# Local attention and two expert layers: pooled products ahead of the local maximum, more places for loads

## Chip, core and metric

One core of a Trainium2 chip runs the whole program. The metric is the device time of one execution in microseconds (us). The engines are TensorE (PE, with its weight loads as PEld), VectorE (DVE), ScalarE (ACT), GpSimd (POOL) and SyncE (SP), which only issues loads and stores.

## What is computed

Attention over 2 batches of 8 heads, 576 positions of 64 values, in two branches that are added: one over queries, keys and values averaged in fours (144 positions), one over the full sequence with a mask that leaves each query the keys less than 4 positions away. Then a dense two-layer block with a squared ReLU, then a mixture of 4 experts weighted by normalised probabilities.

```python
q_d = q.reshape(B, H, Sd, factor, D).mean(axis=3)      # k_d, v_d alike
out_up = np.repeat(sm_attn(q_d, k_d, v_d), factor, axis=2)
mask = np.abs(pos[:, None] - pos[None, :]) < factor
scores = np.where(mask, scale * np.matmul(q, k.transpose(0, 1, 3, 2)), -1e9)
attn = softmax(scores)
x = out_up + np.matmul(attn, v)                        # then (B*S, H*D)
x = (s * np.maximum(x @ w_in, 0) ** 2 + b) @ w_out
out = sum(p[:, e:e+1] * (np.maximum(x @ w1[e], 0) @ w2[e]) for e in range(4))
```

## The kernel before

The attention is cut into 16 units: a unit `u` is one pair of heads (64 + 64 partitions) in one half of the queries of one batch. The first half has 4 tiles of 64 queries, the second 5. Units 0 to 3 and 8 to 11 are first halves: they also load and transpose the keys of their pair and pool its keys and values, which the second-half units 4 to 7 and 12 to 15 use again. Each tile of queries sees a window of 72 keys.

A unit passes through steps, one loop turn apart. `a_step` transposes keys (line 494) and queries (line 512) on TensorE, copies them out of PSUM on ScalarE (kT, line 500; qz, line 519) and sums the queries in fours on VectorE (qd, line 526). `k_step` pools the keys on GpSimd (tk and kd, lines 539 and 541); `v_step` pools the values there (lines 474 and 475). `b_step` opens a PSUM bank with the mask (line 576), adds the local products (line 591), takes the negative local maximum on VectorE (ml, line 599), makes the pooled products (line 605 in first halves, line 615 in second halves) and their maximum (md, line 617), and has ScalarE compute all exponentials (`exps`, line 571). In first halves the pooled products lie in the same bank as the local ones, from column 360 on; in second halves one of two does, the other has a bank of its own. `norm_step` normalises on VectorE (lines 630 to 635), `c_step` transposes the probabilities (line 657, copied out at line 660), `d_step` multiplies them with the values (lines 678 and 685) and joins both branches (lines 694 and 701), and `x_step` splits the sum into two parts for the next layer (lines 713 and 715). There are five PSUM banks for all of these steps.

One loop turn `i` takes its steps in the order b(i-1), a(i), k(i), d(i-3), c(i-2), x(i-3), norm(i-1), v(i-1). Between them stand steps of weight conversion (`prep`: ScalarE at lines 157 and 196, VectorE at lines 161, 167, 175, 186, 199) and, once four units are done, products of the first dense layer (line 316). `keep_warm` adds products on zeros (line 361) whose result nobody reads; their number is fixed by `fill`. The order on each engine is then made by a planner from these priorities and a cost model, except on GpSimd, where it is the order as written. The planner also sets the waits: any two accesses to one PSUM bank by different engines are put in order, whatever columns they touch.

Loads are issued by SyncE in one queue. Turn `i` ends with the keys and queries of unit i+2 (kn, three places; qn, line 443, two places), the values to be pooled of unit i (v4, line 420, one place; in the trace this tile is called v), and the values in windows (vn, lines 458 and 465, three places). Weights are loaded by `load_next` (line 122) into two places.

After the attention the two layers run with TensorE as their pace: dense blocks to about 300 us, experts to the end.

Of the kernel before, what the change touches and what calls it, by code (L numbers as in the profile page):

```python
# [8 lines left out]
F32 = mybir.dt.float32  # L9
# [4 lines left out]
ALU = mybir.AluOpType  # L14
AX = mybir.AxisListType
# [7 lines left out]
def attn_moe_moe_kernel(  # L23
# [14 lines left out]
    nc = tc.nc  # L38
    B, H, S, D = q.shape
# [4 lines left out]
    TQ = 64  # L44
    NTQ = S // TQ
    HALVES = 2
    MX = (NTQ + 1) // 2
# [3 lines left out]
    FAC = 4  # L51
    SD = S // FAC
    ND = SD // 2
# [21 lines left out]
    def window(n):  # L75

        return min(max(n * TQ - FAC, 0), S - W)
# [307 lines left out]
    ap2 = actx.enter_context(tc.tile_pool(name="att2", bufs=2))  # L385
    rctx = ExitStack()
    ap4 = rctx.enter_context(tc.tile_pool(name="att4", bufs=1, side="right"))
# [10 lines left out]
    def unit(u):  # L398
        g, j = divmod(u, NP)
        b, hf = divmod(g, HALVES)  # L400
        return g, j, b, hf

    def tiles(hf):

        return (0, CUT) if hf == 0 else (CUT, NTQ - CUT)
# [6 lines left out]
    def bank():  # L412
        return psa.tile([P, 512], F32, tag="a", name="psa")


    def load_v4(u):
        if u < NU and unit(u)[3] == 0:
            g, j, b, hf = unit(u)
            v4 = ap4.tile([ND, 2, 2, FAC * D], F32, tag="v4", name="v4")
            nc.sync.dma_start(  # L420
                out=v4.rearrange("n a c f -> n (a c) f"),
                in_=v[b, 2 * j : 2 * j + 2].rearrange(
                    "a (c n r) d -> n (a c) (r d)", c=2, r=FAC
                ),
            )
            loaded["v4", u] = v4
# [10 lines left out]
    def load_q(u):  # L437
        if u < NU:
            g, j, b, hf = unit(u)
            n0, m = tiles(hf)  # L440
            gd = m * TQ // FAC
            qn = ap2.tile([MX * TQ // FAC, FAC, 2, D], F32, tag="qn", name="qn")
            nc.sync.dma_start(
                out=qn[:gd],
                in_=q[b, 2 * j : 2 * j + 2, n0 * TQ : (n0 + m) * TQ, :].rearrange(
                    "a (n r) d -> n r a d", r=FAC
                ),
            )
            loaded["q", u] = qn
# [101 lines left out]
    def b_step(u):  # L551

        g, j, b, hf = unit(u)
        n0, m = tiles(hf)
        gd = m * TQ // FAC
        qz, qd = st.pop(("q", u))
        kT = st["kT", j]
        kd = st["kd", j]
        pl = ap2.tile([P, MX, W], F32, tag="pl", name="pl")[:, :m]
        ml = ap2.tile([P, MX, 1], F32, tag="ml", name="ml")[:, :m]  # L560
        both = gd == GB
        pd = ap2.tile([P, 2, SD], F32, tag="pd", name="pd")
        md = ap2.tile([P, 2, 1], F32, tag="md", name="md")
        if both:
            pd, md = pd[:, :1], md[:, :1]
        else:
            pd, md = pd[:gd], md[:gd]
        sm = sums[u % 2]

        def exps(out, ps, m, total):  # L570
            nc.scalar.activation(
                out=out, in_=ps, func=ACTF.Exp, bias=m, scale=1.0, accum_out=total
            )

        ps = [bank()] + ([] if both else [bank()])
        last_pe["att"] = nc.tensor.matmul(
            ps[0][:, : m * W],
            identb.rearrange("p a q -> p (a q)"),
            mask[:, hf * 2 : hf * 2 + m].rearrange("p t w -> p (t w)"),
            start=True,  # L580
            stop=False,
        )
        for _ in range(fill[u] // 448):
            nc.tensor.matmul(
                ps[0][:, : m * W], idle[:, :P], idle[:, : m * W], start=False, stop=False
            )
        for t in range(m):
            k0 = window(n0 + t)
            for a in range(2):
                o = slice(a * D, a * D + D)  # L590
                last_pe["att"] = nc.tensor.matmul(  # L591
                    ps[0][a * TQ : a * TQ + TQ, t * W : t * W + W],
                    qz[o, t * TQ : t * TQ + TQ],
                    kT[o, k0 : k0 + W],
                    start=False,
                    stop=t == m - 1,
                )
        local = ps[0][:, : m * W].rearrange("p (t w) -> p t w", w=W)
        nc.vector.tensor_reduce(out=ml, in_=local, axis=AX.X, op=ALU.max, negate=True)
        pooled = [] if both else [ps[0][:gd, MX * W : MX * W + SD], ps[1][:gd, :SD]]  # L600
        if both:
            pooled = [ps[0][: 2 * gd, MX * W : MX * W + SD]]
            for a in range(2):
                o = slice(a * D, a * D + D)
                last_pe["att"] = nc.tensor.matmul(  # L605
                    ps[0][a * gd : a * gd + gd, MX * W : MX * W + SD],
                    qd[o, :],
                    kd[o, :],
                    start=True,
                    stop=True,  # L610
                )
        else:
            for a in range(2):
                o = slice(a * D, a * D + D)
                last_pe["att"] = nc.tensor.matmul(pooled[a], qd[o, :], kd[o, :], start=True, stop=True)  # L615
        for a in range(len(pooled)):
            nc.vector.tensor_reduce(
                out=md[:, a], in_=pooled[a], axis=AX.X, op=ALU.max, negate=True
            )
        for t in range(m):  # L620
            exps(pl[:, t], local[:, t], ml[:, t], sm[:, t])
        for a in range(len(pooled)):
            exps(pd[:, a], pooled[a], md[:, a], sm[: pd.shape[0], MX + a])
        st["p", u] = pl, pd
# [337 lines left out]
    def side_step():  # L962
# [5 lines left out]

    load_k(0)
    load_q(0)  # L970
    make_mask(0, 1)
    make_mask(1, CUT - 1)
    load_k(1)
    load_q(1)
    keep_warm(bank(), 0, 4096)
    pool_order = ExitStack()
    pool_order.enter_context(tc.manual_schedule(engines={mybir.EngineType.Pool}))
    steps = [
        (b_step, 1),
        (a_step, 0),  # L980
        (k_step, 0),
# [9 lines left out]
    for i in range(last + 1):  # L991
# [13 lines left out]
        for f, lag in steps:  # L1005
            u = i - lag
            if 0 <= u < NU:

                with tc.high_priority(ahead.get(f, 0)) if f in ahead and u < NP else nullcontext():
                    f(u)  # L1010
            if f is x_step and u >= 0 and u % NP == NP - 1:
                slots += l1_steps(0, u // NP) + l2_steps(0, u // NP)
                firsts.append(slots[-FC - KD])
                if u < NP:

                    for _ in range(3):
                        take_slot()
            if f in (k_step, c_step) and slots and i < last:
                take_slot()
            if f in (b_step, k_step, c_step, v_step):  # L1020
                side_step()
        load_k(i + 2)
        load_q(i + 2)
        load_v4(i)
        load_v(i)
        if i == 4:
# [105 lines left out]
```

## Time and profile before

| | |
|---|---|
| median of 3 runs | 696.87 us (695.46 to 697.39) |
| the profiled execution | 696.83 us |
| its span, first to last instruction | 695.0 us |
| TensorE busy | 683.0 us, 98% |
| VectorE busy | 404.8 us, 58% |
| ScalarE busy | 346.3 us, 50% |
| GpSimd busy | 101.2 us, 15% |
| mean granted TensorE clock | 0.993 |

The attention with what is woven into it ends at about 142 us. The share of TensorE's idle time is small, so it has to be looked for in places: the timeline gives each gap with what ended it, and the granted clock tells where TensorE ran at the lower of its two levels. A wait is put down to what came last.

### The profile page before, as it was taken

What the parts mean: (1) busy time and instruction counts of PE and PEld (TensorE: products, weight loads), DVE (VectorE), ACT (ScalarE), POOL (GpSimd) and SP (SyncE); (2) the same over time, 40 slices, a digit from 0 to 9 for tenths busy, and PEclk for the clock granted to TensorE, in tenths of its full rate; (3) what the DMA queues carried; (4) which work ended last, traced back from release to release, by engine and by line L of the source; (5) the groups of instructions that cost most, each with busy time, mean ns of one, the idle gap of its engine ahead of it and who ended that gap; (6) DMA issues with size and microseconds to landing.
All of it is one profiled execution on the core that took longest, in us unless ns stands there. A gap on an engine that the chain in (4) does not pass through costs nothing.

```text
span 695.0 us, 11964 instructions
## 1 busy us (share of the span) xinstructions
PE 683.0 (98%) x4788; PEld 620.2 (89%) x4788; DVE 404.8 (58%) x720; ACT 346.3 (50%) x846; POOL 101.2 (15%) x123
## 2 busy tenths in 40 slices
PE   9989999999999999999999999999999999999997
PEld 5768778899999999999899899999898988998996
DVE  1898847778862434496535636645546456455442
ACT  3768757777965666665534423433334233243220
POOL 4431332100000200103011201201211012010000
PEclk9999989999999999999999999999999999999999
DMA  8784635405410011010210201201101103011012
GB/s 179 200 206 102 110 83 159 141 6 192 166 64 1 0 32 46 16 32 1 62 31 31 70 21 56 67 32 38 54 31 62 30 32 91 3 60 31 1 61 75
DMA packets 54167, 46.43 MB, mean 67 GB/s; under 512 B 32224, under 2 KB 42720, under 8 KB 54112
## 3 DMA queue, kind: packets, MB, share of 16 engines
q1 hardware_dynamic: 54112, 45.67, 23.9%
q8 instruction: 37, 0.61, 0.4%
q14 instruction: 18, 0.15, 0.1%
HBM read 43.31 MB, written 2.36 MB: 66 GB/s over the span
## 4 chain that ended last, share of the span: by engine, by line
PE 92%; DVE 6%; ACT 2%; issue 1%; DVEq 0%; ACTq 0%
PE psm L316 43%; PE psx L863 25%; PE psx L316 13%; PE psa L361 3%; PE psa L657 1%; PE psa L685 1%; PE psa L591 1%; PE psa L678 1%; PE psa L512 1%; PE psa L615 1%; PE psa L494 1%; DVE cv L175 0%; DVE cv L186 0%; PE psa L605 0%; DVE cv L161 0%
## 5 line engine op out<-in xcount | busy, mean ns | idle before, releaser
L316 PE MATMUL psm<-w,h 128*128 128x512 f32 x864 | 208.7, 391 | 0.0
L316 PEld LDWEIGHTS psm<-w,h 128*128 128x128 f32 x864 | 158.5, 188 | 30.0
L863 PE MATMUL psx<-x,w 128*128 128x320 f32 (+1 forms) x768 | 117.8, 296 | 0.0
L863 PEld LDWEIGHTS psx<-x,w 128*128 128x128 f32 x768 | 109.3, 190 | 1.7
L259 POOL TENSOR_TENSOR sw<-raw 128x256 f32<-128x256 f32 x32 | 31.3, 1000 | 411.5 <-DMA raw<-in_moe_w_dram 245.4
L878 ACT COPY r<-psx 128x320 f32<-128x320 f32 (+1 forms) x96 | 38.0, 396 | 92.6 <-PE psx L863 92.2
L881 ACT ACTIVATE h<-r 128x320 fp32r<-128x320 f32 (+1 forms) x96 | 42.0, 444 | 83.6 <-DVE r L892 83.6
L934 DVE SCALAR_TENSOR_TENSOR acc<-psm,pr,acc 128x512 f32<-128x512 f32 x63 | 47.2, 749 | 58.0 <-PE psm L316 58.0
L863 PE MATMUL psx<-t,w 128*128 128x320 f32 (+1 forms) x448 | 80.3, 302 | 0.2 <-DVE r L892 0.2
L892 DVE TENSOR_TENSOR r<-psx,r 128x320 f32<-128x320 f32 (+1 forms) x96 | 43.2, 456 | 58.7 <-PE psx L863 56.7
L863 PEld LDWEIGHTS psx<-t,w 128*128 128x128 f32 x448 | 67.0, 189 | 4.5 <-DVE r L892 0.5
L316 PE MATMUL psm<-x,w 128*128 128x320 f32 (+2 forms) x420 | 68.9, 315 | 0.0
L316 PEld LDWEIGHTS psm<-x,w 128*128 128x128 f32 x420 | 63.8, 193 | 0.9 <-issue 0.8
L882 DVE SCALAR_TENSOR_TENSOR h<-r,h 128x320 fp32r<-128x320 f32 (+1 forms) x96 | 47.7, 502 | 18.5 <-ACT h L881 16.2
L316 PE MATMUL psm<-h,w 128*128 128x256 f32 (+2 forms) x360 | 56.3, 305 | 0.0
L316 PE MATMUL psx<-h,w 128*128 128x384 f32 (+1 forms) x312 | 55.8, 327 | 0.0
L316 PEld LDWEIGHTS psx<-h,w 128*128 128x128 f32 x312 | 52.0, 188 | 0.0
L316 PEld LDWEIGHTS psm<-h,w 128*128 128x128 f32 x360 | 50.8, 190 | 1.0 <-issue 0.7
L316 PE MATMUL psx<-x,w 128*128 128x384 f32 (+2 forms) x252 | 43.1, 320 | 0.0
L316 PEld LDWEIGHTS psx<-x,w 128*128 128x128 f32 x252 | 40.6, 188 | 0.0
L237 DVE TENSOR_TENSOR w<-raw,w 128x1024 fp32r<-128x1024 f32 x16 | 19.5, 1224 | 25.8 <-ACT w L234 25.8
L780 DVE TENSOR_TENSOR h<-r,h 128x384 fp32r<-128x384 f32 (+2 forms) x40 | 21.6, 541 | 20.9 <-ACT h L779 19.6
(105 smaller groups left out, 874.6 us busy)
## 6 DMA issues: line engine op xcount, KB each, us to landing
raw<-in_moe_w_dram SPq DMA_DIRECT2D x32, 512.0 KB
raw<-in_moe_w_in_dram SPq DMA_DIRECT2D x8, 1024.0 KB
raw<-in_moe_w_out_dram SPq DMA_DIRECT2D x8, 1024.0 KB
kn<-in_k_dram SPq DMA_DIRECT2D x8, 288.0 KB
v<-in_v_dram SPq DMA_DIRECT2D x8, 288.0 KB
out_dram<-acc SPq DMA_DIRECT2D x9, 256.0 KB
qn<-in_q_dram SPq DMA_DIRECT2D x8, 160.0 KB
vn<-in_v_dram SPq DMA_DIRECT2D x16, 72.0 KB
```

Source lines behind the costliest of these rows:

```text
L237: nc.vector.tensor_tensor(out=k0[1], in0=source(), in1=f32(k0[0]), op=ALU.subtract)
L259: nc.gpsimd.tensor_tensor(out=operand(out), in0=operand(x), in1=operand(y), op=op)
L316: nc.tensor.matmul(o, stat(ps, kk), mov(pm, kk, i), start=c == 0, stop=c == len(terms) - 1)
L361: nc.tensor.matmul(ps[:, c0:], idle[:, :P], idle[:, :n], start=True, stop=True)
L494: last_pe["att"] = nc.tensor.transpose(psk[:, i * KP : i * KP + KP], kn[:, c * m + i].rearrange("p a d -> p (a d)"), ident[:KP, :KP],)
L780: nc.vector.tensor_tensor(out=h[1], in0=r, in1=f32(h[0]), op=ALU.subtract)
L863: nc.tensor.matmul(ps, s_ap(n, half, a, w, kk), xt[x, pi][b][:, kk], start=first and c == 0, stop=c == len(terms) - 1, skip_group_check=True,)
L878: nc.scalar.copy(t, st[name])
L881: nc.scalar.activation(out=h[0][:, halves[hf]], in_=t, func=ACTF.Relu)
L882: nc.vector.scalar_tensor_tensor(out=h[1][:, halves[hf]], in0=t, scalar=0.0, in1=f32(h[0][:, halves[hf]]), op0=ALU.max, op1=ALU.subtract,)
L892: nc.vector.tensor_tensor(out=st[t], in0=st[name], in1=st[t], op=ALU.add)
L934: nc.vector.scalar_tensor_tensor(out=a, in0=ps, scalar=p_e, in1=a, op0=ALU.mult, op1=ALU.add)
```

## The change

Three edits. In `b_step` the reduce that takes the local maximum moves from ahead of the pooled products to behind them. The loaded queries get three places in place of two, the values to be pooled two in place of one. The space comes from the area that the program reserves for transfer descriptors: 4096 bytes per partition are asked for in place of the default.

```diff
-            v4 = ap4.tile([ND, 2, 2, FAC * D], F32, tag="v4", name="v4")
+            v4 = ap4.tile([ND, 2, 2, FAC * D], F32, tag="v4", name="v4", bufs=2)
...
-            qn = ap2.tile([MX * TQ // FAC, FAC, 2, D], F32, tag="qn", name="qn")
+            qn = ap2.tile([MX * TQ // FAC, FAC, 2, D], F32, tag="qn", name="qn", bufs=3)
...
         local = ps[0][:, : m * W].rearrange("p (t w) -> p t w", w=W)
-        nc.vector.tensor_reduce(out=ml, in_=local, axis=AX.X, op=ALU.max, negate=True)
         pooled = [] if both else [ps[0][:gd, MX * W : MX * W + SD], ps[1][:gd, :SD]]
...
                 last_pe["att"] = nc.tensor.matmul(pooled[a], qd[o, :], kd[o, :], start=True, stop=True)
+        nc.vector.tensor_reduce(out=ml, in_=local, axis=AX.X, op=ALU.max, negate=True)
         for a in range(len(pooled)):
             nc.vector.tensor_reduce(
                 out=md[:, a], in_=pooled[a], axis=AX.X, op=ALU.max, negate=True
             )
...
-    nc = _bacc.Bacc("TRN2", target_bir_lowering=False, num_devices=1)
+    nc = _bacc.Bacc(
+        "TRN2", target_bir_lowering=False, num_devices=1, dynamic_dma_scratch_size=4096
+    )
```

## Rows read from the trace of the kernel before

**Rows 1.** The page, busy time by engine: us, share, instructions.
```profile
PE 683.0 (98%) x4788; PEld 620.2 (89%) x4788; DVE 404.8 (58%) x720; ACT 346.3 (50%) x846; POOL 101.2 (15%) x123
```
**Rows 2.** Busy time by stage, attention and after: engines, granted clock, DMA share, GB/s.
```profile
17.00:142.00 125.00, 118.39 (x1369) 98.49 (x1368) 97.18 (x199) 88.85 (x318) 34.83 (x38) 0.96 0.58 140
142.00:670.00 528.00, 527.81 (x3206) 493.64 (x3202) 297.06 (x498) 249.04 (x505) 59.00 (x65) 1.00 0.15 46
```
**Rows 3.** TensorE's timeline, its six gaps: start, us, operation, idle before and releaser.
```profile
24.00 0.46 PE L605 MATMUL psa<-kd,qd 64*64 64x144 f32 x4 [0.61 <-DVE ml L599]
...
38.76 0.47 PE L615 MATMUL psa<-kd,qd 64*80 64x144 f32 x2 [2.01 <-DVE ml L599]
...
48.09 0.47 PE L615 MATMUL psa<-kd,qd 64*80 64x144 f32 x2 [1.04 <-DVE ml L599]
...
85.68 0.28 PE L576 MATMUL psa<-mask,identb 64*128 64x288 bf16 x1 [0.71 <-ACT pd L571]
...
88.29 0.74 PE L605 MATMUL psa<-kd,qd 64*64 64x144 f32 x4 [1.61 <-DVE ml L599]
...
108.37 0.47 PE L615 MATMUL psa<-kd,qd 64*80 64x144 f32 x2 [0.51 <-DVE ml L599]
```
**Rows 4.** Busy time by stretch within the attention: PE, PEld, DVE, ACT, POOL, clock.
```profile
20.00:50.00 30.00, 26.34 (x325) 20.28 (x323) 28.25 (x50) 20.32 (x75) 12.30 (x11) 0.94 0.78 197
...
40.00:45.00 5.00, 5.00 (x50) 4.02 (x50) 4.75 (x9) 3.40 (x16) 2.35 (x2) 0.66 0.76 176
...
50.00:84.00 34.00, 33.92 (x417) 29.04 (x415) 30.11 (x60) 26.35 (x92) 7.95 (x9) 1.00 0.62 117
84.00:95.00 11.00, 8.68 (x70) 7.03 (x69) 4.80 (x15) 6.25 (x29) 4.42 (x7) 0.69 0.48 111
```
**Rows 5.** VectorE's timeline, two maxima that waited for pooled products.
```profile
19.42 0.31 DVE L617 TENSOR_REDUCE md<-psa 128x1 f32<-128x144 f32 x1 [0.87 <-PE psa L605]
...
31.43 0.31 DVE L617 TENSOR_REDUCE md<-psa 128x1 f32<-128x144 f32 x1 [0.71 <-PE psa L605]
```
**Rows 6.** Who waited for whom, to 200 us: us in total, times, longest.
```profile
ACT pl L571 <- DVE md L617: 7.7, 8, 2.2
```
**Rows 7.** TensorE's timeline, first-layer products at the low and the full clock.
```profile
90.73 3.57 PE L316 MATMUL psm<-x,w 128*128 128x320 f32 x12
...
96.40 2.00 PE L316 MATMUL psm<-x,w 128*128 128x320 f32 x12
```
**Rows 8.** Waits of SyncE's queue and of GpSimd for loads, and the transfer queue.
```profile
SPq L420 <- POOL vd L475: 24.2, 5, 6.9
...
SPq L443 <- PE psa L361: 13.0, 6, 3.8
...
POOL v L474 <- DMA v<-in_v_dram: 4.3, 2, 2.3
...
q1 hardware_dynamic: 54112, 45.67, 23.9%
```
**Rows 9.** Timelines of VectorE and GpSimd, one conversion step with and without pooling beside.
```profile
21.30 2.19 DVE L175 SCALAR_TENSOR_TENSOR cv<-raw,cv 128x1024 int32<-128x1024 int32 x1
...
43.02 1.22 DVE L175 SCALAR_TENSOR_TENSOR cv<-raw,cv 128x1024 int32<-128x1024 int32 x1
...
22.48 1.58 POOL L475 TENSOR_TENSOR vd<-v 72x256 f32<-72x256 f32 x1
```
**Rows 10.** Timelines of GpSimd and TensorE, pooled keys and local products of two units.
```profile
29.06 0.52 POOL L541 TENSOR_TENSOR kd<-tk 128x144 f32<-128x144 f32 x1
...
29.49 0.72 PE L591 MATMUL psa<-kT,qz 64*64 64x72 f32 x16
...
84.97 0.42 POOL L541 TENSOR_TENSOR kd<-tk 128x144 f32<-128x144 f32 x1
...
85.96 0.72 PE L591 MATMUL psa<-kT,qz 64*64 64x72 f32 x16
```

## Prediction

> **What bounds the kernel now.** I read the profile in the order of its stages. The page says that TensorE is busy for 683.0 us of the 695.0 us span [rows 1]; split by stage, it stands still only while the attention runs. From 142 to 670 us it is busy 527.81 of 528 us at full clock, from 17 to 142 us 118.39 of 125 us at a granted clock of 0.96 [rows 2]. So the change, which touches the attention alone, can give back what is lost there and no more. Two things are lost: idle time, and time at the lower of the two clock levels. The TensorE timeline names the idle time. Five gaps end with the reduce of line 599 (ml): 0.61, 2.01, 1.04, 1.61 and 0.51 us, together 5.78 us; one of 0.71 us ends with the exponentials (line 571), which held a PSUM bank [rows 3]. The clock: 0.66 in the stretch from 40 to 45 us, right after the gap of 2.01 us, and 0.69 in the one from 84 to 95 us, which holds the gaps of 0.71 and 1.61 us [rows 4]. A granted 0.66 over 5 us is 1.7 us of full-rate work lost, 0.69 over 11 us is at most 3.4 us (TensorE also idled in it).
>
> Then I asked what stands behind each gap. From 20 to 50 us VectorE is busy 28.25 of 30 us and TensorE 26.34: there TensorE waits because VectorE has too much to do. From 84 to 95 us VectorE is busy 4.80 of 11 us [rows 4]: there the wait is latency, a chain that hops between engines. From 50 to 84 us TensorE is busy 33.92 of 34 us and sets the pace.
>
> **Part 1: pooled products ahead of ml.** Nothing is added or removed: 16 reduces at line 599, 32 products each at lines 605 and 615 stay as they are. Only the order within a unit (one pair of heads, one half of the queries) changes. In `b_step` the pooled product writes columns 360 to 503 of the bank whose columns 0 to 287 or 0 to 359 ml reads, so the wait is for the bank, not for data; it shows as the five gaps of [rows 3]. After the swap TensorE goes from the local products (line 591) straight to the pooled ones, and VectorE gets ml and md together.
>
> First stretch, 17 to 50 us. The gaps of 0.61, 2.01 and 1.04 us (3.66 us) disappear as waits for ml. But VectorE, 94% busy, sets the end of this stretch, and it can only give what it idles itself. It idled for 0.87 and 0.71 us waiting for a pooled product before md, with weight conversion (line 161) queued right behind md [rows 5]. After the swap md follows ml and these 1.58 us go. The rest of TensorE's saved 3.66 us should come back as waits for qd (line 526) or for normalised probabilities (line 632), and the 1.7 us of low clock at 40 to 45 us were spent under a VectorE busy 4.75 of 5 us [rows 4], so I count nothing for them. Bounds: 0, if VectorE finds other gaps, and 3.66 + 1.7 = 5.4 us, if VectorE is not the limit. I take 1.6 us, by VectorE's own rows. From 50 us on TensorE never waits until 84 us, and the loads of these units are issued behind work that moves as well, so I carry the 1.6 us through.
>
> Second stretch, 84 to 95 us. The unit before (u = 9) had its md stuck on VectorE; ScalarE's exponentials waited for md before they could read the same bank, a wait that sums to 7.7 us in eight places [rows 6]. With md right behind ml its exponentials start earlier, the bank comes free, and the gap of 0.71 us goes. The gap of 1.61 us in u = 10 goes because its pooled products are no longer behind ml. Next late would be the key transposes (line 494) and the first-layer products (line 316), whose operands are there, since they follow in the trace without a gap. TensorE then runs on and the clock should not fall. The price of the low clock, 1.2 instead of 2.4 GHz: twelve products of line 316 took 3.57 us there and 2.00 us just after it [rows 7], 1.57 us on one group alone; 3.4 us is the upper end from the granted clock. I take 2.8 us, nearer the upper end, since these products are 3.57 of the 6.8 us (0.31 x 11 / 0.5) at the lower level. Sum of this stretch: 0.71 + 1.61 + 2.8 = 5.1 us; ends 0 (a new wait of the same length keeps the low clock) and 5.7 us.
>
> Third, the gap of 0.51 us at 108 us: 0.5 us; ends 0 and 0.5.
>
> **The cost of the swap.** ml now waits for the pooled products, since they share its bank: 0.46 us for four, from the row of line 605 at full clock (24.00 us) [rows 3]. Where VectorE has a backlog this is hidden: TensorE's gap of 2.01 us before ml was over is far longer than four products. Where it has none, 0.46 us is added before ml and saved before md, so the pair ends no later. I take 0; the ends are 0.46 us for each of the four units of the busy stretch, 1.8 us lost, and the 1.58 us gained above.
>
> The Trainium skill (PSUM — Partial Sum Buffer, section "PSUM bank collisions raise a hardware error") says that two engines must be kept apart by bank and quadrant, whatever columns they touch. By that rule ml cannot start under the pooled products, and the time would be the later one of rival B; the trace agrees that the wait is by bank, with 0.51 to 2.01 us beside disjoint columns.
>
> **Part 2: three places for qn.** SyncE waited 13.0 us in six places for TensorE before it could issue a load of queries [rows 8]; the transposes of line 512 never waited for one. The next load now finds a free place one unit earlier. Nothing on TensorE hangs on that: 0 us. If the cover went it would be one load more in the early traffic, 160 KB ahead of weights at 197 GB/s [rows 4], 0.8 us; below nothing the same 0.8 us, as weights behind the query on the queue are issued earlier. I take 0.
>
> **Part 3: two places for v4.** SyncE waited 24.2 us in five places for GpSimd to finish pooling values [rows 8], with the other value loads (lines 458, 465) and weights (line 122) queued behind. GpSimd's own waits for values sum to 4.3 us. GpSimd is busy 12.30 of 30 and 4.42 of 11 us in the two stretches [rows 4], so pooling earlier frees nothing on TensorE: 0 us. It may move a pooling step onto another VectorE instruction: at 21.30 us line 175 took 2.19 us with line 475 running beside it, against 1.22 us elsewhere [rows 9]. One such meeting more or less is ±1.0 us; I take 0, since the number of pooling steps stays.
>
> **Part 4: the smaller descriptor area.** All data moves on the hardware queue that SyncE feeds, 54112 packets of 54167 [rows 8]. I see nothing that uses the area: 0 us. The trace cannot show it. The Trainium skill (DMA: Bandwidth & Descriptors, "SWDGE vs HWDGE vs iDMA") says that the area holds descriptors of loads issued from GpSimd, of which there are none.
>
> **The sum.** 1.6 + 5.1 + 0.5 = 7.2 us. The profiled execution took 696.83 us (1.8 us around its span), the median of the runs shown is 696.87, so both references agree: 696.8 − 7.2 = 689.6 us.
>
> **The rivals.**
> A. The forecast, 689.6 us, itself likely between 687 and 692.
> B. VectorE takes back the first stretch: ml waiting for the pooled product costs 0.46 us in four busy units, 1.8 us, or the exponentials and qd arrive late at 85 us so that a wait and the low clock stay. For it: 28.25 of 30 us busy. With the first stretch at −0.2 us and the gap of 1.61 us alone gone later, with the 0.5, the gain is 1.9 us; with half the low-clock loss also gone, 3.3 us: 693.5 to 695 us.
> C. The change does not do what it says: other operations move into the places of the removed waits, because the order on each engine is made anew by the planner, and the same idle time stands elsewhere. For it: TensorE had useful work (lines 494, 512, 361) between local and pooled products in most units. About 696.5 us.
> D. Slower: the pooled products, now at the head of TensorE's queue, wait for pooled keys kd (line 541). GpSimd makes kd freshly in eight of the 16 units, in order behind value pooling. In u = 3 kd ends at 29.58 us, local products at 30.21; in u = 10 kd ends at 85.39 us and the local products at 86.68 [rows 10]. The margins are 0.63 and 1.29 us. Decisive point: kd ending later than the local products. If a value pooling (1.26 + 0.72 us, about 2.0 us for both instructions) came between in three units, 6.0 us of waits plus one new low-clock spell of 2.8 us stand against the 5.78 us of ml waits that go, with the two old spells kept: 696.8 + 3.0 = 699.8 us; with every fresh unit of a group of four, 702 us and more. Against it: the other six units have more room, and keys move up with TensorE.
> E. Full gain: all 5.78 + 0.71 us and both clock spells (1.7 + 2.8): 11.0 us, 685.8 us.
>
> **How the numbers follow.** A 0.50, E 0.06, B 0.20, C 0.13, D 0.11. A measurement of this kernel tells 0.3%, 2.1 us, from no change; faster therefore means below 694.8. That holds A, E and some two thirds of B: 0.69. Same: the rest of B, C and the mild end of D: 0.20. Slower: 0.11. The range reaches from E's end, 686, over A, B and C to 697.5; outside it lie D and the tips, under 0.2.
>
> **What would show it.** Right: no idle time on TensorE that ends with ml; md next to ml on VectorE; granted clock of 1.0 between 84 and 95 us; the last attention product about 7 us earlier, and the stages behind it unchanged in length. First stretch wrong: TensorE idle still near 3.7 us there, ended by qd or pl. Wrong altogether: gaps at lines 605 or 615 that end with kd from GpSimd, or a low clock in a new place.

## The result

The changed kernel takes 686.07 us (median of 4, 685.90 to 686.38) beside 697.06 us for the kernel before: a ratio of 0.9851, 95% interval 0.9835 to 0.9867, 11.0 us less. The forecast was 689.6 us with a range of 686.0 to 697.5: the direction and the range held, the time lies at the range's lower edge, and the gain is half as large again as the forecast 7.2 us. The profiled execution took 685.9 us, its span is 684.1 us.

First the page of the changed kernel, then busy time by stage and stretch (us, then each engine's busy us with its instructions: PE, PEld, DVE, ACT, POOL; granted clock, DMA share, GB/s):

```profile
PE 673.0 (98%) x4788; PEld 614.5 (90%) x4788; DVE 404.7 (59%) x720; ACT 345.2 (50%) x846; POOL 103.0 (15%) x123
...
17.00:132.00 115.00, 109.30 (x1391) 93.32 (x1389) 96.26 (x199) 87.93 (x319) 38.03 (x39) 1.00 0.62 150
132.00:659.00 527.00, 526.70 (x3179) 492.61 (x3179) 297.59 (x498) 248.97 (x504) 57.64 (x64) 1.00 0.15 46
...
20.00:50.00 30.00, 24.68 (x335) 19.17 (x332) 28.31 (x49) 21.21 (x81) 12.87 (x11) 1.00 0.79 197
50.00:84.00 34.00, 33.89 (x438) 29.28 (x436) 29.96 (x65) 27.86 (x97) 11.14 (x12) 1.00 0.69 131
84.00:95.00 11.00, 11.00 (x132) 9.75 (x132) 7.59 (x17) 6.98 (x30) 5.74 (x7) 1.00 0.43 104
```

The attention ends 10.9 us earlier and the stages behind it keep their length, as in [rows 2]. From 84 to 95 us TensorE is busy for all 11 us at full clock, against 8.68 us at 0.69 in [rows 4]. But from 20 to 50 us it is busy less than before, 24.68 against 26.34 us, under a VectorE that is as full as it was. And the page holds a surprise: TensorE's own busy time fell by 10.0 us [rows 1], with the same 4788 instructions.

The gaps that stand in the attention in place of those of [rows 3] (start, us, operation; idle before and what ended it):

```profile
23.27 0.46 PE L604 MATMUL psa<-kd,qd 64*64 64x144 f32 x4 [0.40 <-DVE qd L526]
...
33.02 0.46 PE L678 MATMUL psa<-pT,vd 72*64 72x64 f32 x8 [1.40 <-ACT pT L660]
...
41.76 0.41 PE L657 MATMUL psa<-ident,pd 128*72 128x128 f32 x2 [1.31 <-ACT pd L571]
...
44.30 0.47 PE L614 MATMUL psa<-kd,qd 64*80 64x144 f32 x4 [0.18 <-DVE qd L526]
...
49.59 0.30 PE L657 MATMUL psa<-ident,pl 128*72 128x128 f32 x1 [2.03 <-DVE qd L526]
...
126.88 0.50 PE L316 MATMUL psm<-h,w 128*128 128x256 f32 x2 [0.27 <-DVE h L773]
```

No gap ends with ml. Up to 50 us five others, 5.32 us together, took the place of 3.66 us; from 50 to 126 us there is none. The next two answers set the whole attention of before (to 142.76 us) beside that of after (to 131.88 us):

```profile
0.00:142.76 142.76, 134.86 (x1501) 109.46 (x1501) 100.06 (x209) 94.77 (x335) 42.46 (x59) 0.96 0.62 144
```

```profile
0.00:131.88 131.88, 124.98 (x1501) 103.86 (x1501) 99.36 (x209) 93.63 (x335) 45.35 (x59) 1.00 0.67 155
```

TensorE idled 7.90 us and idles 6.90 us: of the 10.9 us only 1.0 us is idle time. The other 9.9 us are work that takes less time. The two spells at the lower clock, both gone, explain at most 5.1 us of it (1.7 and 3.4 us by the granted clock of [rows 4]). The rest had to be looked for in the work itself. The pooled products of second halves (line 615 before, line 614 after), by the same view for one line alone, first before and then after:

```profile
0.00:142.76 142.76, 7.51 (x32) 0.96 0.62 144
```

```profile
0.00:131.88 131.88, 3.81 (x32) 1.00 0.67 155
```

The same 32 instructions (16 products, since one fp32 product is two instructions) are busy for half the time. The timeline of unit 14 shows why, before:

```profile
122.52 0.85 PE L591 MATMUL psa<-kT,qz 64*64 64x72 f32 x20
123.29 0.47 PE L615 MATMUL psa<-kd,qd 64*80 64x144 f32 x2
123.69 0.50 PE L512 MATMUL psa<-ident,qn 80*128 80x80 f32 x4
123.99 0.48 PE L316 MATMUL psm<-x,w 128*128 128x256 f32 x2
124.40 0.47 PE L615 MATMUL psa<-kd,qd 64*80 64x144 f32 x2
124.80 1.46 PE L316 MATMUL psm<-x,w 128*128 128x256 f32 x10
126.18 0.51 PE L678 MATMUL psa<-pT,vd 72*64 72x80 f32 x8
```

and after:

```profile
112.25 0.85 PE L591 MATMUL psa<-kT,qz 64*64 64x72 f32 x20
113.03 0.48 PE L614 MATMUL psa<-kd,qd 64*80 64x144 f32 x4
113.43 0.50 PE L512 MATMUL psa<-ident,qn 80*128 80x80 f32 x4
113.73 1.67 PE L316 MATMUL psm<-x,w 128*128 128x256 f32 x12
115.33 0.51 PE L678 MATMUL psa<-pT,vd 72*64 72x80 f32 x8
```

Read the starts, not the durations. In second halves the second head's pooled product has a bank of its own, did not wait for ml, and went first; the other waited for its turn, 1.1 us later. Each product took 0.40 us from its start to the next start. Side by side all four instructions take the same 0.40 us (113.03 to 113.43): the two heads use different halves of TensorE's rows and share the time. And the dense products in between, 0.41 + 1.38 us when cut in two, take 1.60 us in one run. That is 0.59 us for this unit, and none of it is a wait.

The Trainium skill (TensorE: Matmul & The Clock Gate, "Part 3: Packing small matmuls — row/col tiling") says that a weight load overlaps with products in flight only when it goes to another group of rows, and that small products in different groups of rows run at the same time. The two timelines agree: 0.40 us for one head's two instructions, 0.40 us for both heads' four.

How long each unit took, from the start of its mask product (line 576) to that of the next, in us, for the kernels of this study that matter here (read off the timelines):

| units | before | full change | swap in first halves | swap in second halves | before, pair side by side behind ml |
|---|---|---|---|---|---|
| start of unit 6 | 55.28 | 54.45 | 54.67 | 54.45 | 58.03 |
| 6 | 7.35 | 6.77 | 7.35 | 6.77 | 7.18 |
| 7 | 10.09 | 9.55 | 10.09 | 10.08 | 9.41 |
| 8 | 7.27 | 6.98 | 6.97 | 7.28 | 7.18 |
| 9 | 5.69 | 4.63 | 6.06 | 4.86 | 4.91 |
| 10 | 12.66 | 8.28 | 8.50 | 13.74 | 11.05 |
| 11 | 7.41 | 6.97 | 6.96 | 7.42 | 7.41 |
| 12 | 8.66 | 7.10 | 8.54 | 7.39 | 8.42 |
| 13 | 7.86 | 7.27 | 7.86 | 7.26 | 7.46 |
| 14 | 7.34 | 6.76 | 7.35 | 6.77 | 7.82 |

### The profile page after: what moved, and what is told of

It is laid out like the page before. It is cut to its first block, busy times and chain, and to the rows that moved or that the text cites. A ratio compares the mean times of both kernels' runs of the same rounds, so it can differ in the third digit from the quotient of the medians.

```text
span 684.1 us, 11957 instructions
## 1 busy us (share of the span) xinstructions
PE 673.0 (98%) x4788; PEld 614.5 (90%) x4788; DVE 404.7 (59%) x720; ACT 345.2 (50%) x846; POOL 103.0 (15%) x123
## 3 DMA queue, kind: packets, MB, share of 16 engines
HBM read 43.31 MB, written 2.36 MB: 67 GB/s over the span
## 4 chain that ended last, share of the span: by engine, by line
PE 89%; DVE 7%; ACT 2%; issue 1%; POOL 1%; POOLq 0%; ACTq 0%
PE psm L316 43%; PE psx L863 26%; PE psx L316 13%; PE psa L361 2%; PE psa L591 1%; PE psa L657 1%; DVE cv L175 1%; PE psa L685 1%; PE psa L512 1%; DVE cv L167 1%; PE psa L494 1%; PE psa L678 1%; DVE cv L186 1%; DVE cv L161 0%; DVE pl L632 0%
## 5 line engine op out<-in xcount | busy, mean ns | idle before, releaser
L316 PE MATMUL psm<-x,w 128*128 128x320 f32 (+2 forms) x420 | 66.6, 310 | 0.0
L316 PEld LDWEIGHTS psm<-x,w 128*128 128x128 f32 x420 | 62.3, 189 | 0.3 <-issue 0.2
```

Of the source, the lines that this page charges most:

```text
L316: nc.tensor.matmul(o, stat(ps, kk), mov(pm, kk, i), start=c == 0, stop=c == len(terms) - 1)
```

## The experiments

Diffs are against the full change where nothing else is said.

**Swap alone**, all loads and the descriptor area as before:

```diff
-            v4 = ap4.tile([ND, 2, 2, FAC * D], F32, tag="v4", name="v4", bufs=2)
+            v4 = ap4.tile([ND, 2, 2, FAC * D], F32, tag="v4", name="v4")
...
-            qn = ap2.tile([MX * TQ // FAC, FAC, 2, D], F32, tag="qn", name="qn", bufs=3)
+            qn = ap2.tile([MX * TQ // FAC, FAC, 2, D], F32, tag="qn", name="qn")
...
-        "TRN2", target_bir_lowering=False, num_devices=1, dynamic_dma_scratch_size=4096
+        "TRN2", target_bir_lowering=False, num_devices=1
```

> The swap alone, with the places for loads and the descriptor area as before. Theory (the swap is the whole change; loads hide behind other work): the time of the full change, 686.1 us, within 0.7 us. Rival (part of the gain came from loads that are issued earlier, so that something beside TensorE runs earlier): 688 to 690 us.

Measured: 685.38 us, ratio 0.9847 (0.9831 to 0.9864), the full change's 0.9851 within its interval. The swap is the whole gain. Its profile adds a point on the clock, from 20 to 50 us:

```profile
20.00:50.00 30.00, 26.57 (x339) 20.85 (x338) 27.99 (x53) 21.74 (x81) 11.92 (x11) 0.94 0.80 214
```

The granted clock is 0.94, as low as before, and the kernel is no slower for it. TensorE idles 3.43 us here and loses 1.8 us by the clock (0.06 of 30 us); in the full change it idles 5.32 us at a clock of 1.00. The two come to about the same: under a VectorE that is busy for 28 of 30 us the spell at the lower clock took the place of idle time and cost nothing that the time shows.

**Places alone**, ml ahead of the pooled products as before:

```diff
         local = ps[0][:, : m * W].rearrange("p (t w) -> p t w", w=W)
+        nc.vector.tensor_reduce(out=ml, in_=local, axis=AX.X, op=ALU.max, negate=True)
...
-        nc.vector.tensor_reduce(out=ml, in_=local, axis=AX.X, op=ALU.max, negate=True)
         for a in range(len(pooled)):
```

> The extra places and the smaller descriptor area alone, ml ahead of the pooled products as before. Theory: no change, 697.1 us within 1 us, while SyncE's waits for queries (13.0 us before) and for value pooling (24.2 us) shrink to a few us. Rival (loads matter): 694 to 695 us.

Measured: 697.26 us, ratio 1.0019 (1.0005 to 1.0033): no gain, if anything 0.2% slower. Its waits of SyncE's queue:

```profile
SPq L458 <- PE psa L685: 33.0, 8, 8.0
SPq L420 <- POOL vd L475: 4.2, 2, 3.5
...
SPq L443 <- PE psa L591: 2.3, 1, 2.3
```

The two largest waits of the two loads fell from 24.2 and 13.0 us [rows 8] to 4.2 and 2.3 us. The queue now waits one line further, before the windows of values (line 458), which have three places still.

**Swap in first halves only:**

```diff
-        nc.vector.tensor_reduce(out=ml, in_=local, axis=AX.X, op=ALU.max, negate=True)
+        if both:
+            nc.vector.tensor_reduce(out=ml, in_=local, axis=AX.X, op=ALU.max, negate=True)
```

with the same statement under `if not both:` at its old place.

> The change with the swap in first-half units only (units 0 to 3 and 8 to 11). Theory (two mechanisms: waits for ml with the clock that falls after them, mostly in first halves; and two pooled products of second halves that overlap on TensorE only when they stand next to each other, 0.40 us for each of 8 units): the gap of 1.61 us and the low clock behind it go, the 0.40 us of second halves stay: 691 us, and the pairs of line 615 or its like still stand apart in the timeline, 0.40 us each. Rival (waits alone, as in the prediction, where this part was 5.1 us and the rest of the gain is noise of the new order): 690 us or less only if the first stretch is given back too; otherwise 692 us.

Measured: 691.98 us, ratio 0.9944 (0.9923 to 0.9965), 3.9 us less than before by the ratio. By the table, unit 10 is down to 8.50 us, units 8 and 11 are down by 0.30 and 0.45 us, and units 6, 13 and 14 stand where they stood before, to 0.01 us. So the 0.58 us of a second half belong to its own order. The time alone would fit the rival's 692 us better than the 691 us of the theory; the units decide for the theory. In front of unit 10 a gap of 1.36 us, for a bank, and then one of 0.27 us are left, and no low clock follows them:

```profile
85.14 0.28 PE L576 MATMUL psa<-mask,identb 64*128 64x288 bf16 x1 [1.36 <-ACT pd L571]
...
84.00:95.00 11.00, 9.59 (x114) 8.01 (x114) 6.50 (x18) 7.75 (x33) 3.97 (x6) 1.00 0.43 100
```

**Swap in second halves only**, with `both` and `not both` exchanged:

> The change with the swap in second-half units only (units 4 to 7 and 12 to 15). Theory of the two mechanisms: 8 x 0.40 = 3.2 us from products that now overlap, 0.5 us from the gap at 108 us, some 0.8 us from the first stretch: about 692.5 us, with the low clock after 85 us still there. Rival (waits alone): the removed second-half waits bring 0.5 us, with the first stretch at most 2.1 us: 695 to 696.5 us.

Measured: 693.73 us, ratio 0.9962 (0.9948 to 0.9976), 2.6 us less, nearer to the theory's 692.5 us than to the rival's 695. Units 6, 13 and 14 have their 0.57 to 0.60 us, unit 12 1.27 us, units 8 and 11 nothing. Unit 10 takes 13.74 us: the wait for ml is there,

```profile
87.02 0.57 PE L606 MATMUL psa<-kd,qd 64*64 64x144 f32 x4 [2.64 <-DVE ml L600]
...
84.00:95.00 11.00, 8.36 (x71) 7.20 (x67) 6.04 (x13) 4.39 (x18) 2.96 (x4) 0.69 0.32 79
```

and the low clock behind it. The two halves of the swap sum to 6.5 us, not 11: with each alone a gap is left near 85 us that the full change does not have (1.36 us for a bank with first halves only, 2.64 us for ml here). Why the bank comes late with first halves only is open.

Unit 7 keeps its length here (10.08 us; 9.55 in the full change), though no wait for ml is left in it. Its rows say why: the planner put two dense products between its two pooled products.

```profile
62.51 0.47 PE L616 MATMUL psa<-kd,qd 64*80 64x144 f32 x2
62.91 0.50 PE L316 MATMUL psm<-h,w 128*128 128x256 f32 x2
63.34 0.47 PE L616 MATMUL psa<-kd,qd 64*80 64x144 f32 x2
```

In the full change all four instructions stand together (62.51 to 62.91 us). So what counts in this unit is the neighbour, not the wait.

**Pair side by side, wait kept.** The kernel before, with one line that queues the first head's pooled product and then the second's behind it:

```diff
-                last_pe["att"] = nc.tensor.matmul(pooled[a], qd[o, :], kd[o, :], start=True, stop=True)
+                with tc.issue_after(last_pe["att"].ins) if a else nullcontext():
+                    last_pe["att"] = nc.tensor.matmul(pooled[a], qd[o, :], kd[o, :], start=True, stop=True)
```

> The kernel before, ml ahead of the pooled products in all units and the wait for it kept; only the two pooled products of second halves are made to issue one behind the other, so that both stand behind ml. Theory (two heads' products share TensorE's time when they stand side by side, and a product in the middle of others costs some 0.2 us more): about 0.4 to 0.6 us less in each second-half unit in which TensorE sets the pace (6, 7, 12 to 15), 2.4 to 3.5 us: 693.5 to 694.5 us beside 697, with the waits for ml still there. Rival (the second halves' gain comes from the wait that is removed): 696 to 698 us, no change or slower, since now both products wait.

Measured: 694.12 us (692.93 to 697.05), ratio 0.9973 (0.9959 to 0.9987). That is 1.9 us less by the ratio and 2.5 us by the medians (696.61 us for the kernel before, run with it): short of the 2.4 to 3.5 expected or at its lower end, and against the rival. Unit 13, in which nothing waits, is 0.40 us shorter than before (7.46 against 7.86): four instructions in 0.41 us, with ml still ahead of them. Units 6 and 7 are together 0.85 us shorter (16.59 against 17.44 us), about twice 0.40; singly they don't compare, since two dense products moved from unit 7 to unit 6.

```profile
114.62 0.99 PE L316 MATMUL psm<-h,w 128*128 128x320 f32 x5
115.54 0.48 PE L616 MATMUL psa<-kd,qd 64*80 64x144 f32 x4
115.95 0.50 PE L512 MATMUL psa<-ident,qn 80*128 80x80 f32 x4
```

Unit 14 pays 1.00 us for a new wait for ml, and unit 6 starts 2.75 us late, after two gaps of 2.65 and 2.36 us: now both products wait. The mechanism is shown apart from the removed wait; its price per unit is 0.40 us. The remaining 0.2 us of the 0.59 goes with the dense run, which stays cut in two here (0.92 + 1.20 us in unit 13, 1.93 us in one run in the full change).

**Pair apart, no wait.** The full change, with the second head's pooled product ahead of the local ones, whose heads go second, first:

```diff
+        if not both:
+            nc.tensor.matmul(ps[1][:gd, :SD], qd[D:, :], kd[D:, :], start=True, stop=True)
         for t in range(m):
             k0 = window(n0 + t)
-            for a in range(2):
+            for a in (0, 1) if both else (1, 0):
...
-            for a in range(2):
-                o = slice(a * D, a * D + D)
-                last_pe["att"] = nc.tensor.matmul(pooled[a], qd[o, :], kd[o, :], start=True, stop=True)
+            last_pe["att"] = nc.tensor.matmul(pooled[0], qd[:D, :], kd[:D, :], start=True, stop=True)
```

> The full change, but in the eight second-half units the pooled product of the second head (64 upper rows of the array) goes ahead of the local products, whose heads are taken in the order second, first; the other pooled product stays behind them. No wait comes back and no work is added. Theory (the two heads' products use different halves of TensorE's rows and overlap only side by side): here neither has a neighbour on the other half that it could share time with, so each unit pays about 0.40 us again: 686.1 + 8 x 0.40 = 689.3 us. Rival (the unforeseen gain came from the new order elsewhere, not from neighbours): 686 us within 0.7 us.

Measured: 691.19 us (688.54 to 692.53), ratio 0.9918 (0.9891 to 0.9944), 4.7 us more than the full change by the ratios, more than the 3.2 expected. The profile is of the fastest run, and most of its loss is not the pair: from unit 6 to unit 15 it takes 4.47 us more than the full change, of which units 9, 10 and 12, with three gaps (1.36 and 0.27 us around the start of unit 10, 1.42 us in unit 12), hold 3.42 us and units 6, 7, 13 and 14 hold 1.07 us. The price of the pair is read from these four. Units 6 and 7 are 0.40 and 0.39 us longer than in the full change (7.17 and 9.94 us), as expected. Units 13 and 14 only 0.13 and 0.15 us (7.40 and 6.91 us), and the rows say why:

```profile
115.11 0.32 PE L576 MATMUL psa<-mask,identb 64*128 64x360 bf16 x1
115.12 0.47 PE L588 MATMUL psa<-kd,qd 64*80 64x144 f32 x2
115.52 0.85 PE L593 MATMUL psa<-kT,qz 64*64 64x72 f32 x20
```

The early product (upper rows) starts 0.01 us after the mask product (lower rows) and hides its 0.25 us. In units 6 and 7 a product on zeros that fills all rows stands between them.

**The same, local products first head first** (the loop `for a in range(2)` unchanged):

> As the run before, but the local products keep the order first head, second head, so that the early pooled product (upper rows) has a local product of the lower rows right behind it. Theory (different rows overlap, whichever products they are): most of the 0.40 us is hidden again, 686 to 687.5 us. Rival (only two pooled products of equal length overlap, or distance alone costs): 689.3 us as the run before.

Measured: 690.64 us, ratio 0.9910 (0.9889 to 0.9931). The expectation failed: units 6, 13 and 14 take 7.17, 7.41 and 6.91 us, as in the run before. A lower-row local product right behind the upper-row pooled one hid nothing, nor did the upper-row local product ahead of the other pooled one. Unit 13:

```profile
109.74 0.47 PE L588 MATMUL psa<-kd,qd 64*80 64x144 f32 x2
110.14 0.85 PE L593 MATMUL psa<-kT,qz 64*64 64x72 f32 x20
110.92 0.47 PE L614 MATMUL psa<-kd,qd 64*80 64x144 f32 x2
```

So different halves of the rows are not enough. Why the mask product shares time with it and the local products don't was not tried further. The rows offer a candidate that no run tests: the pooled and the mask products, which shared time, have weights wider than 64 columns (64*80, 64*128), the local ones have 64 (64*64).

**Fewer products on zeros.** In the full change TensorE is busy throughout from 50 to 84 us, and some of its products there are read by nobody. Two kernels leave them out from unit 6 and from unit 5 on:

```diff
-    fill = [1408 if u < NP else 512 if u < 2 * NP + 2 else 0 for u in range(NU)]
+    fill = [1408 if u < NP else 512 if u < 6 else 0 for u in range(NU)]
```

> The full change with the products on zeros of units 6 to 9 left out (their result is not read). They lie in the stretch from 50 to 84 us, in which TensorE is busy throughout and sets the pace, together about 6 us by the sum of single durations and some 3 us by starts. Theory (TensorE is the bound there and the clock holds by the other work): 683 to 684.5 us. Rival (VectorE, busy 30 of 34 us, takes over, or the clock falls): 685.5 us or more, with gaps that end with VectorE.

> As the run before with unit 5 left without them as well: some 0.6 us of TensorE's work less, but partly in the stretch to 50 us which VectorE bounds. Theory: 0 to 0.6 us below the run before. Rival (VectorE is the bound already): no difference from it, or a clock that falls near 60 us and 1 to 2 us more.

Measured: 687.23 us (0.9867, 0.9850 to 0.9883) and 688.51 us (0.9882, 0.9859 to 0.9904). No gain: the rivals came. With units 6 to 9 left out:

```profile
76.21 0.46 PE L604 MATMUL psa<-kd,qd 64*64 64x144 f32 x4 [1.22 <-DVE qd L526]
...
80.60 0.41 PE L657 MATMUL psa<-ident,pd 128*72 128x128 f32 x2 [1.31 <-ACT pd L571]
...
84.00:95.00 11.00, 11.00 (x95) 9.87 (x94) 6.21 (x15) 6.27 (x24) 4.58 (x6) 0.75 0.34 78
```

Unit 10 starts at 80.95 us in place of 82.38, but unit 6 already started 1.36 us ahead (53.09 us in place of 54.45; the swap alone, with all products on zeros, starts it at 53.38). From unit 6 to unit 10 the time is the same, 27.86 against 27.93 us: units 6 to 8 are 2.42 us shorter, and unit 9, with the two gaps shown, is 2.35 us longer. Then follows a granted clock of 0.75, and unit 10 takes 11.22 us in place of 8.28. The work that was left out came back as gaps, and the clock that fell with them took more.

**Values by turns**, the two loops of lines 675 to 678 exchanged:

```diff
         for a in range(2):
-            o = slice(a * D, a * D + D)
-            for c in range(2):
+        for c in range(2):
+            for a in range(2):
+                o = slice(a * D, a * D + D)
```

> The full change, with the four products of pooled probabilities and pooled values of each unit taken by turns (first head, second head) in place of two of the first and two of the second. If heads that write different halves of the output rows overlap as those that read different halves of the array's rows do: 0.05 to 0.1 us less in each of 16 units, 685 to 685.5 us. Otherwise 686.1 us.

Measured: 686.08 us, ratio 0.9854 (0.9835 to 0.9874): no difference. No kernel of the study is clearly faster than the full change; the swap alone is as fast.

## Why the prediction was right or wrong

**What bounds the kernel, and the rule that only the attention counts:** right in place, wrong in kind. The whole gain lies in the attention, 10.9 of 10.9 us. But "can give back what is lost there and no more" counted idle time and low clock as all that can be lost, and took TensorE's work as fixed. This is the step that failed. Busy time was 134.86 us for work that takes 124.98 us in the new order, and the clock is at most 5.1 us of that.

**First stretch, 1.6 us forecast:** 0.83 us at the start of unit 6 in the profile of the full change, 1.90 us in that of the swap alone (53.38 us), whose compute engines work in nearly the same order. The mechanism held in the main: the three gaps that ended with ml became five that end with qd, pT and pd, longer together, and VectorE stayed as full. That VectorE sets the end is still read from its busy time: no run took work off it, and two of the five gaps, 2.71 us, end with ScalarE. On VectorE ml and md stand together, with conversion right behind them, where md stood alone in [rows 5]:

```profile
18.58 0.46 DVE L615 TENSOR_REDUCE ml<-psa 128x4 f32<-128x288 f32 x1 [0.65 <-PE psa L604]
18.95 0.30 DVE L617 TENSOR_REDUCE md<-psa 128x1 f32<-128x144 f32 x1
19.17 0.68 DVE L161 TENSOR_SCALAR cv<-cv 128x1024 f32<-128x1024 f32 x1
```

Counting nothing for the first spell at the low clock was right, as the swap alone shows. The sum of 3.66 + 1.7 us of waits and clock would have been wrong by 3.5 to 4.5 us.

**50 to 84 us, nothing forecast:** units 6 to 8 became 1.41 us shorter (0.58, 0.54, 0.29), though TensorE had no gap there. Forecasting 0 from "busy 33.92 of 34 us" was wrong.

**Second stretch, 5.1 us forecast:** units 9 and 10 became 1.06 and 4.38 us shorter, 5.44 us. Unit 10 gave its gap of 1.61 us and 2.8 us for the clock (12.66 − 8.28 − 1.61 = 2.77, with the few tenths in it that units 8 and 11 show for their closer order): near the price taken from one group at either level. The gap of 0.71 us went as said; ScalarE's waits for md fell from 7.7 us [rows 6] to

```profile
ACT pl L571 <- DVE md L617: 4.8, 6, 1.9
```

**Third, 0.5 us forecast:** units 11 to 14 became 0.44, 1.56, 0.59 and 0.58 us shorter, 3.17 us. The gap of 0.51 us is part of unit 12's.

**The term that was missing** is so 1.41 us and 2.7 us, about 4 us: pooled products next to each other, and dense runs not cut in two. For units 6, 13 and 14 (1.75 us) it is shown: the swaps by halves put their 0.6 us each on the second halves' order, and the pair behind ml shows 0.40 us of it without any removed wait. For units 7 and 12 it is read from the traces: unit 7's 0.54 us go where its pair stands apart, and unit 12's 1.56 us are the gap of 0.51, 0.40 for the pair and some 0.65 for runs of lines 316 and 685 that stood cut before. The 0.30 to 0.45 us of units 8 and 11 belong to the first halves' order, but no run splits the amount; there the local and the pooled products now follow directly, and the group of key transposes is whole.

**Cost of the swap, 0:** ml waited for the pooled products in some units (0.65 us in the row above), with no VectorE time lost on balance: 28.25 and 28.31 us busy from 20 to 50 us.

**Places and descriptor area, 0:** right, by the run with the places alone; the 0.2% that it may cost is inside what was allowed for.

**The rivals:** C (same idle time elsewhere) was half right, 7.90 against 6.90 us, and yet the time fell, since idle time was not what it cost. D did not come: no gap ends with kd. E gave the right time, 685.8 us, by a wrong sum: it takes back all waits and both spells, where TensorE still idles 6.90 us and the first spell was free. That the forecast's range held is luck as well: its lower end was E's 686, which stood there by that wrong sum; the 4 us of the missing term were in no term of the forecast.

## What to carry to other kernels

An engine that is busy from end to end may still be slow: compare the start-to-start time of the same group of instructions in different neighbourhoods, and where two products use different halves of the array, try them side by side (here it gave 0.40 us a pair; the local products, though in the other half, hid nothing). Move a wait and it shows what it kept apart; ask not only who waits, but what stands between instructions because of the wait. In a stretch that another engine fills, removed waits and low clock were worth little more than what that engine idled; in the stretch bound by latency they were worth all of it, the clock's fall included.

## What the runs showed of the hardware

One fp32 product of 64 rows by 144 columns took 0.40 us from its start to the next one's; two of them in different halves of the rows, side by side, took 0.40 us together. With the pair apart, a product of the upper rows hid the mask product of the lower rows ahead of it (started 0.01 us apart), but not the local products of the lower rows behind it (0.40 us from start to start).

With 0.71 and 1.61 us of idle time close together TensorE's granted clock was 0.69 over the stretch from 84 to 95 us that holds them, and with 2.64 us alone as well; with 1.36 and 0.27 us, in the run with first halves only, it stayed at 1.00. The length of a gap alone does not tell: with one of 1.39 us, in the run with the pair behind ml, the clock was 0.84 over the same stretch, and in the full change it stayed at 1.00 through gaps of 1.40, 1.31 and 2.03 us.

```profile
89.05 0.46 PE L605 MATMUL psa<-kd,qd 64*64 64x144 f32 x4 [1.39 <-DVE ml L599]
...
84.00:95.00 11.00, 9.61 (x117) 8.02 (x114) 5.66 (x16) 6.78 (x31) 6.06 (x8) 0.84 0.38 97
```
